# W products of both head parities in one burst, attention tiles in one PSUM ring, new ranks in the planner

## The chip, the cores and the metric

The kernel runs on one core of a Trainium2 chip. The metric is the device time of one execution in microseconds. Three runs of the kernel before took 285.99, 286.09 and 287.48 us; the median is 286.09 us.

## The reference, cut to what matters

There are 8 batches of 8 heads, 576 tokens and a head size of 64. In each head 32 "pack" queries first attend over the tokens, and the 576 token queries then attend over the 32 packed rows. Behind that stands an MLP with a gated activation:

```
p_packed = softmax(p @ k.T / 8) @ v              # 32 x 64 for each head
att      = softmax(q @ p_packed.T / 8) @ p_packed
x        = att, heads side by side               # 4608 x 512
h        = x @ w_in                              # 512 -> 2048
out      = (h * sigmoid(beta * h)) @ w_out       # 2048 -> 512
```

## The kernel before, in words

**Tiling.** Work goes batch by batch. The 8 heads are laid out as four columns c of two parities r: head 2c + r has partitions 64r to 64r + 63. The 576 tokens are split into 512 (main) and 64 (rest). The kernel never forms att: since p_packed is the value matrix of the second attention, att @ w_in equals the softmax weights times a small matrix W = p_packed @ w_in, which is 32 rows for each head, 256 rows by 2048 columns for a batch. So the MLP's first product has 256 rows to sum over instead of 512.

**Steps of one batch b**, with the names that the profile and the prediction use:

- k, q, v are loaded by SP (plan_loads) and cast to bf16 by POOL. `tr` transposes k and q on TensorE (tiles kT_ps, qT_ps), DVE copies them out (L279). `trr` and `rk`, `rq` do the same for the 64 rest tokens (remT_ps, L311, L313).
- `s1` and `s1r` are the scores of the pack queries (s1_ps, s1r_ps), `e1` their exp on ACT (L338, L357), `z1` the sums (z1_ps: a 128x64 tile of ones, once for each parity), `i1` the reciprocal on DVE (L390), `pun` the product with v (pp_ps), `pp` its scaling (L410).
- `s2` and `s2r` are the scores of the tokens against the packed rows, one tile for each parity (64x32 tiles of the array). `e2` is their exp (L450, L453), `z2` the sums (z2_ps), then ln and exp(-x) on ACT (L472, L474, L483) for the reciprocal, and `A2` the weights on DVE (L488).
- `w` is W: for each quarter n of the 2048 columns and each parity r, four matmuls of a 64x32 tile with 512 columns, one for each c, into one PSUM tile (w_ps). DVE multiplies it by beta into W_bf (`W`, L550, 0.68 us).
- `h` is W by A2 (two matmuls for each of 16 blocks ft, h_ps; `hr` for the rest tokens). ACT applies Silu (`g`, L578, L598).
- `o` is g by w_out in four tiles of 128 tokens, 16 matmuls each (o_ps), and a fifth for the rest tokens of two batches (g_rem). DVE copies each out (`take`, L636), and SP stores it.

In the profile all matmuls have line L164 and all transposes L169, the lines of two helpers; the tiles tell them apart. z1_ps and z2_ps are both shown as z_ps, s1_ps and s2_ps as s_ps.

**The order.** Every step is a Task with an engine, an assumed duration, what it depends on, and a rank. Planner.run plays the engines against assumed times, and emits on each free engine the ready task of lowest rank. The result is a fixed order for each engine. A task that opens a PSUM tile (`takes`) needs the oldest buffer of a ring to have been given back (`ends`). There are three rings: "h" with 2 buffers, "o" with 2 and "att" with 4. Before, h, hr, remT, s1r, z1 and pp share the ring "h", and all else of attention the ring "att". ACT has two table sets: exp (with ln) and silu. The rule for a switch is

```
if other and (mode == "silu" or not same) and not (mode == "exp" and soon):
```

where `other` are the tasks that could start now and need the other set, `same` those of the present set, and `soon` the exp tasks that come ready within 1.6 us. While the planner's clock is under 36 us (WARM_UNTIL), idle TensorE gets filler matmuls (warm_ps).

**Ranks before.** Attention of batch b has 100b + 5 to 100b + 12, h has 100b + 50, o has 100b + 260 and more. h(b) depends on the o tiles of batch b - 2, since g has two buffers.

Of the kernel before, what the change touches and what calls it, by code (L numbers as in the profile page):

```python
# [8 lines left out]
B, H, S, D = 8, 8, 576, 64  # L9
# [6 lines left out]
bf16 = mybir.dt.bfloat16  # L16
# [5 lines left out]
NC = 4  # L22
FT = DFF // 128
SM = 512
SR = 64
# [3 lines left out]
HOP_US = 0.2  # L29
LAND_US = 2.0  # L30
WARM_UNTIL = 36.0


class Task:

    __slots__ = ("engine", "us", "fn", "deps", "rank", "takes", "ends", "table", "end", "slot", "left", "ready", "users", "key")

    def __init__(self, engine, us, fn, deps, rank, takes, ends, table):  # L40
        self.engine, self.us, self.fn, self.deps, self.rank = engine, us, fn, deps, rank
        self.takes, self.ends, self.table = takes, ends, table
        self.end, self.slot, self.users, self.key = None, None, [], None
        self.left, self.ready = 0, 0.0


class Planner:
# [7 lines left out]

    def add(self, engine, us, fn, deps=(), rank=0, takes=None, ends=(), table=None):
        t = Task(engine, us, fn, [d for d in deps if d is not None], rank, takes, ends, table)
        self.tasks.append(t)
        return t

    def run(self):
# [9 lines left out]
        now, todo = 0.0, len(self.tasks)  # L71

        def room(t):
            if t.takes is None:
                return True
            n, opened = self.rings[t.takes]
            return len(opened) < n or (opened[-n][0] is not None and opened[-n][0] <= now + 1e-9)

        def start(t):
            nonlocal todo  # L80
            if t.takes is not None:
                t.slot = [None]
                self.rings[t.takes][1].append(t.slot)
            t.fn()
            t.end = now + t.us
            free[t.engine] = t.end
            for o in t.ends:
                o.slot[0] = t.end + HOP_US
            land = LAND_US if t.engine == "SP" else HOP_US
            for u in t.users:  # L90
                u.left -= 1
                u.ready = max(u.ready, t.end + (0.0 if u.engine == t.engine else land))
                if not u.left:
                    ready[u.engine].append(u)
            ready[t.engine].remove(t)
            todo -= 1

        while todo:
# [24 lines left out]
            if not moved:  # L123
                times = [x for x in free.values() if x > now + 1e-9]
                times += [t.ready for q in ready.values() for t in q if t.ready > now + 1e-9]
                times += [
                    o[-n][0] for n, o in self.rings.values() if len(o) >= n and o[-n][0] and o[-n][0] > now + 1e-9
                ]
                assert times, [(t.key, t.engine, room(t), t.ready - now) for q in ready.values() for t in q] + [[d.key for d in t.deps if d.end is None] for t in self.tasks if t.end is None and t.left][:9]
                now = min(times)  # L130


class Kernel:
# [128 lines left out]
    def plan_attention(self, b):  # L262
        nc = self.nc
        rank = 100 * b + 5
        st = self.t
# [18 lines left out]
        for x in "kq":  # L284
            old = [("s1", b - 1, i) for i in range(2)] if x == "k" else [("s2", b - 1, i) for i in range(3)]
            for i in range(2):
# [10 lines left out]
        def transpose_rest():  # L297
            st[b, "r", "ps"] = ps = self.ps_h.tile([128, 1024], bf16, tag="h", name="remT_ps")
            for xi, x in enumerate("kq"):
                for u in range(2):  # L300
                    self.tp(
                        ps[:, 256 * xi + 128 * u : 256 * xi + 128 * u + 128],
                        st[b, x][:, 2048 + 128 * u : 2048 + 128 * u + 128],
                        self.identr[:],
                    )

        def evacuate_rest(x):
# [11 lines left out]
            ("trr", b), "PE", 0.24, transpose_rest,  # L319
            [("cast", b, "k", 2), ("cast", b, "q", 2), ("s1r", b - 1), ("T", b, "q", 1)], rank + 1, takes="h",  # L320
        )
# [23 lines left out]
        def scores1_rest():  # L345
            st[b, "s1r"] = ps = self.bank("s1r_ps")
            for u in range(2):
# [6 lines left out]
        def exp1_rest():  # L354
# [4 lines left out]
        old = [("z1", b - 2), ("pun", b - 2)]  # L359
        s1r = self.task(("s1r", b), "PE", 0.12, scores1_rest, [("rk", b), ("pT",)] + old, rank + 2, takes="h")  # L360
        s1 = [
# [6 lines left out]
        e1 = [  # L368
            self.task(("e1", b, i), "ACT", 0.62, lambda i=i: exp1(i), [s1[i], s1r], rank + 2, ends=[s1[i]], table="exp")
            for i in range(2)  # L370
        ]
        e1.append(self.task(("e1r", b), "ACT", 0.56, exp1_rest, [s1r], rank + 2, ends=[s1r], table="exp"))
# [19 lines left out]
        def packed():  # L392
            st[b, "pun"] = ps = self.bank("pp_ps")
            v = st[b, "v"]
# [11 lines left out]
        def normalize1():  # L406
# [9 lines left out]

        z1 = self.task(("z1", b), "PE", 0.5, sums1, e1 + [("pp", b - 2)], rank + 3, takes="h")
        i1 = self.task(("i1", b), "DVE", 0.97, invert1, [z1], rank + 3, ends=[z1])
        old = [("s2", b - 2, i) for i in range(3)] + [("w", b - 2, n) for n in range(8)]
        pun = self.task(  # L420
            ("pun", b), "PE", 0.75, packed,
            e1 + [z1] + [("cast", b, "v", i) for i in range(3)] + old, rank + 4, takes="h",
        )
        self.task(("pp", b), "DVE", 0.6, normalize1, [i1, pun], rank + 4, ends=[pun])


        def scores2(i):
            st[b, "s2", i] = ps = self.att("s2_ps")
            for c in range(NC):
                self.mm(  # L430
                    ps[32 * c : 32 * c + 32, :],
                    st[b, "pp"][64 * i : 64 * i + 64, c, :],
                    st[b, "q", "T"][64 * i : 64 * i + 64, c, 0:SM],
                    pos=(64 * i, 32 * c),
                )

        def scores2_rest(r):
            st[b, "s2r", r] = ps = self.att("s2r_ps")
            for c in range(NC):
                self.mm(  # L440
                    ps[32 * c : 32 * c + 32, 0:SR],
                    st[b, "pp"][64 * r : 64 * r + 64, c, :],
                    st[b, "q", "T"][64 * r : 64 * r + 64, c, SM:S],
                    pos=(64 * r, 32 * c),
                )

# [48 lines left out]
        oldA = [("h", b - 2, ft) for ft in range(FT)] + [("hr", b - 2, 0), ("hr", b - 2, 1)]  # L495
        e2, s2r = [], []
        for i in range(2):
            s2 = self.task(("s2", b, i), "PE", 0.25, lambda i=i: scores2(i), [("pp", b), ("s2", b, i - 1)] + tq + oldE, rank + 5, takes="att")
            e2.append(
                self.task(  # L500
                    ("e2", b, i), "ACT", 0.62, lambda i=i: exp2(i), [s2] + e2[:1], rank + 5, ends=[s2], table="exp"
                )
            )
        for r in range(2):
            s2r.append(
                self.task(
                    ("s2", b, 2) if r else None, "PE", 0.1, lambda r=r: scores2_rest(r),
                    [("pp", b), ("rq", b), ("s2", b, 1)] + s2r + oldE, rank + 6, takes="att",
                )
            )  # L510
        e2r = [
            self.task(None, "ACT", 0.25, lambda r=r: exp2_rest(r), [s2r[r], e2[0]], rank + 6, ends=[s2r[r]], table="exp")
            for r in range(2)
# [19 lines left out]

        def fused_w(m):
            n, r = m // 2, m % 2
            st[b, "w", m] = ps = self.att("w_ps")
            for c in range(NC):
                self.mm(
                    ps[32 * c : 32 * c + 32, :],
                    st[b, "pp"][64 * r : 64 * r + 64, c, :],  # L540
                    self.w_in_bf[64 * r : 64 * r + 64, c, 512 * n : 512 * n + 512],
                    pos=(64 * r, 32 * c),
                )

# [8 lines left out]

        for m in range(8):
            w = self.task(
                ("w", b, m), "PE", 0.27, lambda m=m: fused_w(m),
                [("pp", b), ("w_in", m // 2), ("beta", m // 2), ("w", b, m - 1)] + oldA, rank + 7, takes="att",
            )
            self.task(("W", b, m), "DVE", 0.68, lambda m=m: scaled_w(m), [w, ("W", b, m - 1)], rank + 7, ends=[w])


    def plan_mlp(self, b):
        nc = self.nc
        st = self.t
        rank = 100 * b + 50

# [307 lines left out]
```

## Time and profile before

| | |
|---|---|
| median of three runs | 286.09 us |
| profiled execution | 285.96 us |
| its span, first to last instruction | 284.2 us |
| mean granted TensorE clock | 0.992 |
| TensorE (PE) busy | 269.2 us, 95% |
| ScalarE (ACT) busy | 151.5 us, 53% |
| VectorE (DVE) busy | 127.4 us, 45% |
| GpSimd (POOL) busy | 59.9 us, 21% |
| ACT table loads | 16 |

Times are microseconds unless marked ns. PE's busy time counts modelled ends, so what a matmul costs is read from the distance between starts. PEld is the weight load, which overlaps PE. In a row of groups stand: line, engine, operation, tile written and tiles read, shapes, count, then busy time and mean ns of one, and the idle time of the engine ahead of them with what ended most of it. In a timeline row stand: start, length, engine, line, operation, tiles, shapes, count, and in brackets a wait ahead of it.

### The profile page before, as it was taken

How to read it: one execution, taken by the hardware profiler on the slowest of the kernel's cores; microseconds unless marked ns; L12 is line 12 of the kernel's file. 1: busy time of each engine (PE TensorE's matmuls, PEld its weight loads, DVE VectorE, ACT ScalarE, POOL GpSimd, SP SyncE). 2: the span in 40 equal slices, each digit the busy share in tenths (PEclk: the TensorE clock that was granted, in tenths of full speed). 3: DMA queues.
4: the chain of work that ended last, by engine and by line, in shares of the span. 5: the costliest groups of instructions: out<-in, count | busy, mean ns of one | idle time of the engine just before them, and what ended most of it. 6: DMA issues, size and time to landing. Idle time of an engine off the chain costs nothing.

```text
span 284.2 us, 5670 instructions
## 1 busy us (share of the span) xinstructions
PE 269.2 (95%) x2382; PEld 138.8 (49%) x2382; DVE 127.4 (45%) x232; ACT 151.5 (53%) x280; POOL 59.9 (21%) x58
## 2 busy tenths in 40 slices
PE   7957999999999999999999999999999999989993
PEld 6954555345553446444553446434563445524441
DVE  6636536893156504581146502492055802381110
ACT  1637476626638465636627467355646366387500
POOL 4117560143081006300170005400063000000000
PEclk9999799999999999999999999999999999999999
DMA  6999999989939701991149510791021011100022
GB/s 217 303 350 367 299 327 379 319 238 317 290 112 294 214 37 40 256 311 44 39 145 325 178 40 37 228 334 52 0 76 70 9 35 38 75 37 2 10 101 74
DMA packets 47737, 47.02 MB, mean 165 GB/s; under 512 B 14289, under 2 KB 38881, under 8 KB 47713
## 3 DMA queue, kind: packets, MB, share of 16 engines
q1 hardware_dynamic: 47712, 46.68, 54.2%
q8 instruction: 18, 0.29, 0.5%
q14 instruction: 7, 0.05, 0.1%
HBM read 37.23 MB, written 9.44 MB: 164 GB/s over the span
## 4 chain that ended last, share of the span: by engine, by line
PE 76%; DMA 13%; DVE 5%; SPq 3%; POOL 1%; issue 1%; POOLq 0%; DVEq 0%
PE o_ps L164 42%; PE h_ps L164 17%; PE w_ps L164 5%; DMA w_out<-in_moe_w_out_dram 4%; DMA q<-in_q_dram 4%; DMA w_in<-in_moe_w_in_dram 3%; PE hr_ps L164 2%; DMA k<-in_k_dram 2%; PE z_ps L164 2%; PE s_ps L164 2%; PE qT_ps L169 2%; PE kT_ps L169 2%; DVE o_sb L636 2%; SPq L219 2%; DVE A2T L488 1%; PE pp_ps L164 1%
## 5 line engine op out<-in xcount | busy, mean ns | idle before, releaser
L164 PE MATMUL o_ps<-w_out_bf,g_main 128*128 128x512 bf16 x512 | 131.9, 380 | 0.7 <-DVE o_sb L636 0.3
L578 ACT ACTIVATE g_main<-h_ps 128x512 bf16<-128x512 f32 x128 | 71.2, 595 | 59.4 <-PE h_ps L164 59.1
L164 PEld LDWEIGHTS <-g_main 128*128 128x128 bf16 x512 | 45.2, 98 | 52.1 <-issue 9.0
L164 PE MATMUL h_ps<-A2T,W_bf 128*128 128x512 bf16 x256 | 69.1, 382 | 0.4 <-ACT g_main L578 0.4
L636 DVE COPY o_sb<-o_ps 128x512 f32<-128x512 f32 x36 | 24.5, 688 | 95.5 <-PE o_ps L164 95.5
L550 DVE TENSOR_TENSOR W_bf<-w_ps,beta_bc 128x512 bf16<-128x512 f32 x64 | 40.6, 684 | 19.6 <-PE w_ps L164 19.6
L164 PEld LDWEIGHTS <-W_bf 128*128 128x128 bf16 x512 | 32.2, 98 | 30.2 <-issue 5.4
L239 POOL CAST k_bf<-k 128x2048 bf16<-128x2048 f32 x7 | 13.3, 1893 | 119.7 <-PE remT_ps L169 105.4
L450 ACT ACTIVATE E2T<-s_ps 128x512 bf16<-128x512 f32 x16 | 8.7, 595 | 35.9 <-PE s2r_ps L164 29.2
L164 PE MATMUL w_ps<-w_in_bf,pp 64*32 64x512 bf16 x256 | 21.5, 393 | 3.1 <-POOL w_in_bf L786 1.6
L179 ACT ACT_TABLE_LOAD x16 | 20.5, 1283 | 1.0 <-PEq L858 0.7
L164 PEld LDWEIGHTS <-pp 64*32 64x32 bf16 x384 | 6.9, 89 | 27.5 <-issue 23.1
L164 PE MATMUL warm_ps<-identr 128*128 128x128 bf16 x165 | 15.0, 244 | 1.9 <-DVE bones L681 1.9
L239 POOL CAST v_bf<-v 128x2048 bf16<-128x2048 f32 x7 | 13.3, 1893 | 15.1 <-issue 8.4
L164 PE MATMUL o_ps<-w_out_bf,g_rem 128*128 128x512 bf16 x64 | 16.1, 380 | 0.0
L279 DVE COPY kT<-kT_ps 128x1024 bf16<-128x1024 bf16 x15 | 9.8, 685 | 11.5 <-PE kT_ps L169 11.5
L488 DVE TENSOR_TENSOR A2T<-E2T,rz 128x512 bf16<-128x512 bf16 (+1 forms) x24 | 14.7, 648 | 0.2 <-ACT rz L483 0.2
L164 PEld LDWEIGHTS <-identr 128*128 128x128 bf16 x165 | 12.2, 111 | 4.9 <-DVE bones L681 1.9
L239 POOL CAST q_bf<-q 128x2048 bf16<-128x2048 f32 x7 | 13.3, 1893 | 2.8 <-DMA q<-in_q_dram 2.8
L483 ACT ACTIVATE rz<-rz 128x512 f32<-128x512 f32 (+1 forms) x24 | 12.6, 523 | 0.8
L598 ACT ACTIVATE g_rem<-hr_ps 128x512 bf16<-128x512 f32 x16 | 8.9, 595 | 4.8 <-PE hr_ps L164 4.8
L169 PEld LDWEIGHTS <-k_bf 128*128 128x128 bf16 x144 | 9.4, 98 | 3.9 <-issue 0.3
(67 smaller groups left out, 205.1 us busy)
## 6 DMA issues: line engine op xcount, KB each, us to landing
out_dram<-o_sb SPq DMA_DIRECT2D x32, 256.0 KB, 2.4
k<-in_k_dram SPq DMA_DIRECT2D x7, 1024.0 KB, 6.7
q<-in_q_dram SPq DMA_DIRECT2D x7, 1024.0 KB, 8.4
v<-in_v_dram SPq DMA_DIRECT2D x7, 1024.0 KB, 7.8
w_in<-in_moe_w_in_dram SPq DMA_DIRECT2D x4, 1024.0 KB, 9.9
w_out<-in_moe_w_out_dram SPq DMA_DIRECT2D x4, 1024.0 KB, 8.3
k<-in_k_dram SPq DMA_DIRECT2D x2, 512.0 KB, 5.5
k<-in_k_dram SPq DMA_DIRECT2D x16, 64.0 KB, 6.3
```

Source lines behind the costliest of these rows:

```text
L164: return self.nc.tensor.matmul(out, lhsT, rhs, start=start, stop=stop, tile_position=pos, skip_group_check=True)
L169: return self.nc.tensor.matmul(out, in_, ident, is_transpose=True, skip_group_check=True)
L179: self.nc.scalar.preload_act_table_set(SETS[mode])
L239: self.copy[engine](o[:, 0:2048].rearrange("p (t h d) -> p h t d", t=4, h=8)[:, h], t[:, 0:2048].rearrange("p (h t d) -> p h t d", h=8, t= ...
L279: self.copy[engine](st[b, x, "T"][:, 2 * i : 2 * i + 2, 0:SM], st[b, x, "ps", i][:].rearrange("p (c n) -> p c n", c=2),)
L450: nc.scalar.activation(st[b, "E2"][:, i, 0:SM], st[b, "s2", i][:], AF.Exp, scale=SCALE)
L483: nc.scalar.activation(rz, rz, AF.Exp, scale=-1.0)
L488: nc.vector.tensor_tensor(part(st[b, "A2"], i), part(st[b, "E2"], i), part(st[b, "rz2"], i), ALU.mult)
L550: nc.vector.tensor_tensor(st[b, "W"][:, r, cols], st[b, "w", m][:], self.beta_bc[:, cols], ALU.mult)
L578: nc.scalar.activation(st[b, "g"][:, ft, :], st[b, "h", ft][:], AF.Silu)
L598: nc.scalar.activation(st[b // 2, "gr"][:, 8 * half : 8 * half + 8, o : o + 64], st[b, "hr", half][:].rearrange("p (f n) -> p f n", f=8), ...
L636: nc.vector.tensor_copy(o[:], st[b, "o", t][:])
```

## The change

- `w` becomes one task for each quarter n (WN = 1), which takes two buffers of the ring (`count=2`) and issues eight matmuls, parities alternating inside each c. Each of the two buffers is given back by its own evacuation `W`.
- `s2` becomes one task for both parities with two buffers, and `s2r` likewise, also with the parities alternating.
- The ten matmuls of `z1` alternate between the parities, where all five of one came before all five of the other.
- The tiles of `trr`, `s1r`, `z1` and `pun` move from the ring "h" to the ring "att", which keeps four buffers. Only h and hr (and two small tiles at the start) are left in "h".
- `e1` of batch b waits for the first `e2` of batch b - 1, from batch 2 on.
- Attention's ranks go from 100b + 5 to 100b - 30, those of h from 100b + 50 to 100b - 300. s2r has rank + 5 instead of + 6.

The planner's ring test looks at `count` buffers, and a task can end one buffer of several. The diff, cut to its core:

```diff
 def room(t):
-    return len(opened) < n or (opened[-n][0] is not None and opened[-n][0] <= now + 1e-9)
+    for i in range(len(opened) - n, len(opened) - n + t.count):
+        if i >= 0 and (opened[i][0] is None or opened[i][0] > now + 1e-9):
+            return False
+    return True
...
 def plan_attention(self, b):
-    rank = 100 * b + 5
+    rank = 100 * b - 30
...
-    st[b, "r", "ps"] = ps = self.ps_h.tile([128, 1024], bf16, tag="h", name="remT_ps")
+    st[b, "r", "ps"] = ps = self.att("remT_ps", bf16)
...
-    st[b, "s1r"] = ps = self.bank("s1r_ps")
+    st[b, "s1r"] = ps = self.att("s1r_ps")
...
-    self.task(("e1", b, i), "ACT", 0.62, lambda i=i: exp1(i), [s1[i], s1r], rank + 2, ends=[s1[i]], table="exp")
+    self.task(("e1", b, i), "ACT", 0.62, lambda i=i: exp1(i), [s1[i], s1r, ("e2", b - 1, 0) if b > 1 else None], rank + 2, ends=[s1[i]], table="exp")
...
 def sums1():
-    st[b, "z1"] = ps = self.bank("z1_ps")
-    for r in range(2):
-        for t in range(5):
+    st[b, "z1"] = ps = self.att("z1_ps")
+    for t in range(5):
+        for r in range(2):
...
-    st[b, "pun"] = ps = self.bank("pp_ps")
+    st[b, "pun"] = ps = self.att("pp_ps")
...
-def fused_w(m):
-    n, r = m // 2, m % 2
-    st[b, "w", m] = ps = self.att("w_ps")
+def fused_w(n):
+    for r in range(2):
+        st[b, "w", 2 * n + r] = self.att("w_ps")
     for c in range(NC):
-        self.mm(ps[32 * c : 32 * c + 32, :], ...
+        for r in range(2):
+            self.mm(st[b, "w", 2 * n + r][32 * c : 32 * c + 32, :], ...
...
-for m in range(8):
+for n in range(0, 4, WN):
     w = self.task(
-        ("w", b, m), "PE", 0.27, lambda m=m: fused_w(m),
-        [("pp", b), ("w_in", m // 2), ("beta", m // 2), ("w", b, m - 1)] + oldA, rank + 7, takes="att",
-    )
-    self.task(("W", b, m), "DVE", 0.68, lambda m=m: scaled_w(m), [w, ("W", b, m - 1)], rank + 7, ends=[w])
+        ("w", b, n), "PE", 0.15 + 0.25 * WN, lambda n=n: [fused_w(n + i) for i in range(WN)],
+        [("pp", b), ("w", b, n - WN)] + [(x, n + i) for x in ("w_in", "beta") for i in range(WN)] + oldA,
+        rank + 7, takes="att", count=2 * WN,
+    )
+    for i in range(2 * WN):
+        m = 2 * n + i
+        self.task(("W", b, m), "DVE", 0.68, lambda m=m: scaled_w(m), [w, ("W", b, m - 1)], rank + 7, ends=[(w, i)])
...
 def plan_mlp(self, b):
-    rank = 100 * b + 50
+    rank = 100 * b - 300
```

More of the change, by code (lines that the diff above doesn't have):

```diff
@@ L31, with __init__ @@
 WARM_UNTIL = 36.0
+WN = 1
 class Task:
-    __slots__ = ("engine", "us", "fn", "deps", "rank", "takes", "ends", "table", "end", "slot", "left", "ready", "users", "key")
-    def __init__(self, engine, us, fn, deps, rank, takes, ends, table):
+    __slots__ = ("engine", "us", "fn", "deps", "rank", "takes", "count", "ends", "table", "end", "slot", "left", "ready", "users", "key")
+    def __init__(self, engine, us, fn, deps, rank, takes, count, ends, table):
         self.engine, self.us, self.fn, self.deps, self.rank = engine, us, fn, deps, rank
-        self.takes, self.ends, self.table = takes, ends, table
+        self.takes, self.count, self.table = takes, count, table
+        self.ends = [e if isinstance(e, tuple) else (e, 0) for e in ends]
         self.end, self.slot, self.users, self.key = None, None, [], None
@@ L54, in __init__, with add @@
         self.switch, self.filler = switch, filler
-    def add(self, engine, us, fn, deps=(), rank=0, takes=None, ends=(), table=None):
-        t = Task(engine, us, fn, [d for d in deps if d is not None], rank, takes, ends, table)
+    def add(self, engine, us, fn, deps=(), rank=0, takes=None, count=1, ends=(), table=None):
+        t = Task(engine, us, fn, [d for d in deps if d is not None], rank, takes, count, ends, table)
         self.tasks.append(t)
@@ L81, in start @@
             if t.takes is not None:
-                t.slot = [None]
-                self.rings[t.takes][1].append(t.slot)
+                t.slot = [[None] for _ in range(t.count)]
+                self.rings[t.takes][1].extend(t.slot)
             t.fn()
@@ L86, in start @@
             free[t.engine] = t.end
-            for o in t.ends:
-                o.slot[0] = t.end + HOP_US
+            for o, i in t.ends:
+                o.slot[i][0] = t.end + HOP_US
             land = LAND_US if t.engine == "SP" else HOP_US
@@ L284, in plan_attention @@
         for x in "kq":
-            old = [("s1", b - 1, i) for i in range(2)] if x == "k" else [("s2", b - 1, i) for i in range(3)]
+            old = [("s1", b - 1, i) for i in range(2)] if x == "k" else [("s2", b - 1, i) for i in range(2)]
             for i in range(2):
@@ L319, in plan_attention @@
             ("trr", b), "PE", 0.24, transpose_rest,
-            [("cast", b, "k", 2), ("cast", b, "q", 2), ("s1r", b - 1), ("T", b, "q", 1)], rank + 1, takes="h",
+            [("cast", b, "k", 2), ("cast", b, "q", 2), ("s1r", b - 1), ("T", b, "q", 1)], rank + 1, takes="att",
         )
@@ L359, in plan_attention @@
         old = [("z1", b - 2), ("pun", b - 2)]
-        s1r = self.task(("s1r", b), "PE", 0.12, scores1_rest, [("rk", b), ("pT",)] + old, rank + 2, takes="h")
+        s1r = self.task(("s1r", b), "PE", 0.12, scores1_rest, [("rk", b), ("pT",)] + old, rank + 2, takes="att")
         s1 = [
@@ L495, in plan_attention @@
         oldA = [("h", b - 2, ft) for ft in range(FT)] + [("hr", b - 2, 0), ("hr", b - 2, 1)]
[L496 to L510, printed above, removed]
+        s2 = self.task(
+            ("s2", b, 0), "PE", 0.3, lambda: scores2("s2", 0, SM), [("pp", b)] + tq + oldE, rank + 5, takes="att", count=2
+        )
+        e2 = [
+            self.task(("e2", b, i), "ACT", 0.62, lambda i=i: exp2(i), [s2], rank + 5, ends=[(s2, i)], table="exp")
+            for i in range(2)
+        ]
+        s2r = self.task(
+            ("s2", b, 1), "PE", 0.14, lambda: scores2("s2r", SM, S),
+            [("pp", b), ("rq", b), s2] + oldE, rank + 5, takes="att", count=2,
+        )
         e2r = [
-            self.task(None, "ACT", 0.25, lambda r=r: exp2_rest(r), [s2r[r], e2[0]], rank + 6, ends=[s2r[r]], table="exp")
+            self.task(None, "ACT", 0.25, lambda r=r: exp2_rest(r), [s2r, e2[0]], rank + 6, ends=[(s2r, r)], table="exp")
             for r in range(2)
```

49 lines of the change are left out of this document (20 added, 29 removed).

## The prediction

> **What bounds the kernel now.** I read the page first, for the span and the busy shares.
>
> ```profile
> span 284.2 us, 5670 instructions
> ## 1 busy us (share of the span) xinstructions
> PE 269.2 (95%) x2382; PEld 138.8 (49%) x2382; DVE 127.4 (45%) x232; ACT 151.5 (53%) x280; POOL 59.9 (21%) x58
> ```
>
> The profiled execution took 285.96 us, 1.76 us more than its span and 0.13 us less than the median of 286.09 us; the sum below is made against 285.96. TensorE is the candidate, but its busy share is modelled, so the next view is the table of windows, one window per batch in the middle of the run (columns: window, its length, then busy time and count of PE, PEld, DVE, ACT, POOL; granted clock; DMA share; GB/s).
>
> ```profile
> 60.00:93.00 33.00, 33.00 (x298) 16.24 (x299) 16.86 (x30) 19.18 (x36) 10.31 (x10) 1.00 0.89 252
> ...
> 191.00:224.00 33.00, 32.87 (x280) 15.80 (x279) 13.85 (x26) 17.94 (x35) 6.66 (x6) 1.00 0.15 50
> ```
>
> PE has no gap in these windows and its clock is full (1.00), while ACT works 18 to 19 of 33 us and DVE 14 to 17. So over the middle of the run the time is what the PE instructions cost, one behind the other, and a microsecond taken out of PE comes off the end, provided PE still finds work. What each of them costs is read from the starts in the PE timeline (start, length, instruction, count), not from the lengths.
>
> ```profile
> 151.84 0.40 PE L164 MATMUL w_ps<-w_in_bf,pp 64*32 64x512 bf16 x4
> 152.17 1.04 PE L164 MATMUL o_ps<-w_out_bf,g_main 128*128 128x512 bf16 x4
> 153.14 0.40 PE L164 MATMUL w_ps<-w_in_bf,pp 64*32 64x512 bf16 x4
> 153.47 1.04 PE L164 MATMUL o_ps<-w_out_bf,g_main 128*128 128x512 bf16 x4
> 154.44 0.41 PE L164 MATMUL w_ps<-w_in_bf,pp 64*32 64x512 bf16 x8
> 154.78 1.04 PE L164 MATMUL o_ps<-w_out_bf,g_main 128*128 128x512 bf16 x4
> 155.75 0.40 PE L164 MATMUL w_ps<-w_in_bf,pp 64*32 64x512 bf16 x4
> ...
> 160.44 1.03 PE L164 MATMUL o_ps<-w_out_bf,g_rem 128*128 128x512 bf16 x4
> 161.30 1.03 PE L164 MATMUL h_ps<-A2T,W_bf 128*128 128x512 bf16 x4
> ```
>
> Four full-array matmuls that are left alone take 161.30 - 160.44 = 0.86 us, so one pass of 512 columns is 0.216 us. The four W products of one head parity (64x32 tiles side by side) hold PE for 152.17 - 151.84 = 0.33 us, a pass and 0.11 us more, and the four o matmuls ahead of the next burst take 153.14 - 152.17 = 0.97, another 0.11 us over 0.86. A burst of one parity thus costs 0.44 us for 0.216 us of streaming; the rest is paid at its two edges. The burst of eight at 154.44 happens to hold both parities, and takes 0.34 us (to 154.78) with the same edge of 0.11 after it (155.75 - 154.78 = 0.97): 0.45 us for twice the work. That is the saving the change can have.
>
> **The W bursts.** I counted the bursts in the PE timeline from the first W product of batch 1 to the last of batch 6; these are the two ends of the list.
>
> ```profile
> 54.13 0.40 PE L164 MATMUL w_ps<-w_in_bf,pp 64*32 64x512 bf16 x4
> ...
> 223.51 0.40 PE L164 MATMUL w_ps<-w_in_bf,pp 64*32 64x512 bf16 x4
> ```
>
> There are 41: 35 of four, 5 of eight and one of twelve. Their cost is 35 x 0.44 = 15.40, 5 x 0.45 = 2.25, and 0.45 + 0.216 = 0.67 for the twelve: 18.3 us. After the change each batch has four bursts of eight: 24 x 0.45 = 10.8. Gain 7.5 us, all on the path as PE has no gap there. If the planner places two pairs back to back when the ring is empty, two edges (0.22 us) go per such place: at one a batch another 1.3 us, the low end. What is new is that parities alternate inside the burst, which no row shows. If each pair of row halves ran one after the other, a burst would take a pass more: 24 x 0.216 = 5.2 us back; below nothing it can't go, since a burst of eight already runs in one pass. I take 0.45, since the nearest row (154.44) has all eight tiles at work at once.
>
> Batch 7 is apart, because PE has little o work left to put between its bursts:
>
> ```profile
> 249.71 0.45 PE L164 MATMUL w_ps<-w_in_bf,pp 64*32 64x512 bf16 x8
> 250.91 0.50 PE L164 MATMUL w_ps<-w_in_bf,pp 64*32 64x512 bf16 x8 [0.75 <-ACT rz L472]
> 251.74 0.87 PE L164 MATMUL w_ps<-w_in_bf,pp 64*32 64x512 bf16 x8 [0.33 <-ACT rz L474]
> 252.55 1.08 PE L164 MATMUL h_ps<-A2T,W_bf 128*128 128x512 bf16 x4
> 253.62 0.40 PE L164 MATMUL w_ps<-w_in_bf,pp 64*32 64x512 bf16 x4
> 254.22 0.40 PE L164 MATMUL w_ps<-w_in_bf,pp 64*32 64x512 bf16 x4 [0.20 <-DVE W_bf L550]
> 254.55 1.04 PE L164 MATMUL h_ps<-A2T,W_bf 128*128 128x512 bf16 x4
> ```
>
> From 249.71 to 254.55 are 4.84 us, of which 0.86 is the four h matmuls; 3.98 us go to W products and to waits (0.75 + 0.33 + 0.20 = 1.28) for the ring. Afterwards attention of batch 7 no longer waits for the h ring, so it falls into the time of silu(6), where o work covers it: 4 x 0.45 = 1.8, a gain of 2.2 us (from 0.9 with the waits left to 2.2). Batch 0 gains nothing: its W products wait for w_in.
>
> **z1 and s2.** These are the rows of one batch.
>
> ```profile
> 178.70 0.55 PE L164 MATMUL z_ps<-E1T,ones 128*64 128x128 bf16 x10
> 179.18 0.76 PE L164 MATMUL pp_ps<-E1T,v_bf 128*128 128x64 bf16 x20
> ...
> 181.60 0.41 PE L164 MATMUL s_ps<-qT,pp 64*32 64x512 bf16 x8
> 181.82 0.21 PE L164 MATMUL s2r_ps<-qT,pp 64*32 64x64 bf16 x8
> 181.97 1.04 PE L164 MATMUL o_ps<-w_out_bf,g_main 128*128 128x512 bf16 x4
> ```
>
> The ten z1 matmuls take 0.48 us. Ten passes of 128 columns in a row would be 10 x 0.054 + 0.11 = 0.65, five pairs 5 x 0.054 + 0.11 = 0.38: the two halves overlap already, so the new order can bring 0.10 a batch at most and lose 0.17 if it breaks the overlap; I take half the gain, 0.4 us in eight batches (from -1.4 to 0.8). The eight s2 products run already in one pass (181.82 - 181.60 = 0.22), with s2r right behind: nothing to gain, and 0.22 us a batch to lose (two more edges, 1.5 us in seven) if s2r must wait for its two buffers and o work comes between. I take nothing, because z1 and pun give their buffers back before s2 can start.
>
> **The ring, the ranks and the tables.** remT, s1r, z1 and pp move from the two h buffers to the ring of four, and h gets the lowest rank numbers. No instruction is added, and W needs two free buffers at once, which DVE empties one after the other. The costs are in waits. Behind a waiting W burst on PE stand h, o and attention of the next batch; behind W's evacuation on DVE stand i1, pp, A2 and the o copies. I cost them at nothing because the o matmuls of a batch (64 x 0.216 = 13.8 us) are ready by then; their price without that cover is a rival below. ACT gets nothing from shared tables that would show:
>
> ```profile
> L578 ACT ACTIVATE g_main<-h_ps 128x512 bf16<-128x512 f32 x128 | 71.2, 595 | 59.4 <-PE h_ps L164 59.1
> L179 ACT ACT_TABLE_LOAD   x16 | 20.5, 1283 | 1.0 <-PEq L858 0.7
> ```
>
> There are 16 loads, the first and two a batch less one at the end. An exp stretch and a silu stretch per batch stay, so 16 is about the least afterwards too; and ACT sits 59.1 us waiting for h from PE. The Trainium skill ("ScalarE: Activation LUTs", What ACT_TABLE_LOAD costs) puts a switch at about 2.66 us with a drain; the rows here have 1.283 us, and by the page's price the sum stays as it is, for no load goes. What does move is the gap inside one exp stretch:
>
> ```profile
> 182.05 1.08 ACT L450 ACTIVATE E2T<-s_ps 128x512 bf16<-128x512 f32 x2 [5.10 <-PE s2r_ps L164]
> ...
> 186.19 1.28 ACT L179 ACT_TABLE_LOAD   x1
> ```
>
> ACT waited 5.10 us there between the first and the second softmax of the same batch. With e1 of the next batch behind e2 this gap falls away, which shortens ACT's chain, not PE's work. Of the queues that work is moved past, SP's loads and POOL's casts come due some us earlier; POOL waits 105.4 us for transposes ahead of k casts, so the data is there long before:
>
> ```profile
> L239 POOL CAST k_bf<-k 128x2048 bf16<-128x2048 f32 x7 | 13.3, 1893 | 119.7 <-PE remT_ps L169 105.4
> ```
>
> The first 44 us are set by loads, which stay: the first o matmuls wait for this cast and its DMA.
>
> ```profile
> 43.57 1.68 DVE L796 TENSOR_SCALAR w_out_bf<-w_out,rbeta 128x512 bf16<-128x512 f32 x4 [3.07 <-DMA w_out<-in_moe_w_out_dram]
> ```
>
> Attention of batch 1 may slip into PE's free time before that (a gain of about 1 us), or its table switch may hold up the last silus of batch 0 (two loads of 1.283, a loss of up to 2.6 us); I take nothing.
>
> **The sum.** 7.5 + 2.2 + 0.4 = 10.1 us; 285.96 - 10.1 = 275.9, and 276.0 against the median.
>
> **The rivals.** First, *evacuation takes over*:
>
> ```profile
> L550 DVE TENSOR_TENSOR W_bf<-w_ps,beta_bc 128x512 bf16<-128x512 f32 x64 | 40.6, 684 | 19.6 <-PE w_ps L164 19.6
> ```
>
> DVE needs 2 x 0.684 = 1.37 us per pair, and the ring now also carries four more tiles a batch. Where PE waits in each of batches 1 to 6 as it does in batch 7 (1.28 us), 7.7 us come back: 283.7. Against it: DVE is under half busy and the middle windows have no PE gap even with single bursts. The Trainium skill ("TensorEngine Tiling (Array Packing)", PSUM Bottleneck) says that packing speeds the array and not the emptying of PSUM, which can then become the bound; this case's trace shows it only in batch 7. A part of these waits, 2 to 5 us, gives 278 to 281. Second, *the alternating parities serialise*: 276.0 + 5.2 = 281.2. Against it speaks the row at 154.44.
>
> Third, slower: *the table ping-pong*. The rule in Planner.run leaves silu mode as soon as any exp task can start. With s1r, z1 and pp out of the h ring, e1 or s2 of the next batch can come ready in the middle of silu(b); ACT then loads exp, does its 4.1 us (182.05 to 186.19), and loads silu. If e1 and e2 come at different times, that is two loads (2.57 us) more per batch, and h stands still meanwhile. PE feels it only when the o work runs out. It decides from 10.1 / 7 = 1.44 us uncovered per batch; with all of 2.57 uncovered in seven batches, 18 us come back: 294. For it: the old order kept the two stretches apart by the h ring, and the new one has only e1's wait on e2. Against it: ACT has 59.1 us of slack, and a stop of 6.7 us is under the 13.8 us of o work. Fourth, *nothing moves*, because ACT's chain of switches and waits sets the period once PE is lighter: about 285.9.
>
> **How the numbers follow.** The forecast (274.5 to 277.5) has 0.46. Below it 0.14: pairs back to back at two places a batch (2.6) and an early batch 1 (1.0) reach 272.4. A part of the waits, or s2r apart, 0.18; serialised 0.03; evacuation in full 0.05; nothing moves 0.02; slower by ping-pong 0.12. The range 272.4 to 283.8 leaves out the last two and little besides. Half a per cent, 1.4 us, is about what a measurement can tell here. Faster takes all the cases that end below 284.7, 0.86; same 0.02; slower 0.12.
>
> **What would show it.** Right: W products of batches 1 to 6 in bursts of eight, 0.34 us from start to next start; no PE gap in windows of about 31.5 us a batch; 16 to about 20 table loads; z1 at 0.38 to 0.48. Wrong: PE waits on W_bf or on s and z tiles' readers in the chain of waits (evacuation), bursts of 0.55 (serialised), 28 or more table loads with PE waits on g_main (ping-pong), or a last h batch that starts no sooner.

## The result, and the profile after

The changed kernel takes 276.62 us (median of four, 275.46 to 278.71), beside 286.39 us for the kernel before in the same session: a ratio of 0.966 (95% interval 0.959 to 0.973). Forecast were 276.0 us and a range of 272.4 to 283.8. The total was right. The experiments show that the reason given for it was only half of the mechanism.

The profiled execution took 278.71 us, the slowest of the four, so it shows 7.25 us less than the profile of before and not the 9.8 us between the medians. First come the page's head and two windows from the middle (window, its length, busy time and count of PE, PEld, DVE, ACT, POOL; granted clock; DMA share; GB/s):

```profile
span 276.8 us, 5707 instructions
PE 260.0 (94%) x2394; PEld 138.7 (50%) x2394; DVE 131.8 (48%) x232; ACT 173.0 (62%) x296; POOL 60.6 (22%) x58
...
60.00:93.00 33.00, 33.00 (x332) 17.23 (x331) 21.58 (x37) 25.91 (x43) 14.21 (x12) 1.00 1.00 271
...
191.00:224.00 33.00, 33.00 (x286) 15.53 (x270) 16.36 (x29) 23.07 (x43) 1.00 (x2) 1.00 0.11 41
```

PE is as full as before, at full clock in these windows, but ACT now works 23 to 26 of 33 us where it worked 18 to 19. Now z1 and two W bursts in the timeline of PE (start, length, instruction, count):

```profile
125.33 0.47 PE L167 MATMUL z_ps<-E1T,ones 128*64 128x128 bf16 x10
125.74 0.76 PE L167 MATMUL pp_ps<-E1T,v_bf 128*128 128x64 bf16 x20
...
132.57 0.41 PE L167 MATMUL w_ps<-w_in_bf,pp 64*32 64x512 bf16 x8
132.91 1.90 PE L167 MATMUL o_ps<-w_out_bf,g_main 128*128 128x512 bf16 x8
134.74 0.41 PE L167 MATMUL w_ps<-w_in_bf,pp 64*32 64x512 bf16 x8
135.08 1.25 PE L167 MATMUL o_ps<-w_out_bf,g_main 128*128 128x512 bf16 x5
```

A pair takes 132.91 - 132.57 = 0.34 us and the edge behind it 134.74 - 132.91 - 8 x 0.216 = 0.10: 0.44 us, as forecast. Batches 1 to 6 hold 24 such bursts and no other. z1 takes 0.41 us where it took 0.48.

What was not forecast is on ACT. Groups (busy us, mean ns, then idle us before them and what ended most of it), and a stretch of ACT's timeline:

```profile
L182 ACT ACT_TABLE_LOAD x32 | 41.1, 1283 | 1.3 <-PEq L853 0.7
L573 ACT ACTIVATE g_main<-h_ps 128x512 bf16<-128x512 f32 x128 | 71.2, 595 | 46.5 <-PE h_ps L167 46.0
```

```profile
120.98 0.60 ACT L573 ACTIVATE g_main<-h_ps 128x512 bf16<-128x512 f32 x1 [0.43 <-PE h_ps L167]
121.59 1.28 ACT L182 ACT_TABLE_LOAD   x1
122.89 0.55 ACT L360 ACTIVATE E1T<-s1r_ps 64x128 bf16<-64x128 f32 x2
123.47 1.08 ACT L341 ACTIVATE E1T<-s_ps 128x512 bf16<-128x512 f32 x2
124.57 1.28 ACT L182 ACT_TABLE_LOAD   x1
125.86 1.09 ACT L573 ACTIVATE g_main<-h_ps 128x512 bf16<-128x512 f32 x2
127.39 1.08 ACT L573 ACTIVATE g_main<-h_ps 128x512 bf16<-128x512 f32 x2 [0.45 <-PE h_ps L167]
128.50 1.28 ACT L182 ACT_TABLE_LOAD   x1
129.79 1.09 ACT L445 ACTIVATE E2T<-s_ps 128x512 bf16<-128x512 f32 x2
```

The table loads doubled, from 16 to 32. The first softmax of the next batch breaks into the silus of this one, then the second does, each with a load on both sides. This is the ping-pong that the prediction described, and it costs the path nothing visible: PE waits for no g_main after 50 us (its one named wait from there on is 1.7 us for an o copy), and ACT's waiting for h falls from 59.1 to 46.0 us. In return attention runs ahead. The end of the run:

```profile
221.55 0.41 PE L167 MATMUL w_ps<-w_in_bf,pp 64*32 64x512 bf16 x8
221.89 1.90 PE L167 MATMUL o_ps<-w_out_bf,g_main 128*128 128x512 bf16 x8
223.72 0.41 PE L167 MATMUL w_ps<-w_in_bf,pp 64*32 64x512 bf16 x8
...
227.23 0.63 PE L167 MATMUL w_ps<-w_in_bf,pp 64*32 64x512 bf16 x16
...
243.37 1.10 PE L167 MATMUL hr_ps<-A2T,W_bf 128*128 128x64 bf16 x32
```

Batch 7 has its W at 221.55 (249.71 before), inside the silus of batch 6 and without a wait, and its last h products at 243.37 (266.2 before). Behind them 128 o matmuls run to the end in one row.

**An account of PE's time.** From the first o matmul to the last, I priced every instruction by its start-to-start time (0.216 us for a pass of 512 columns and so on), each W pass at 0.216 and each change of the tile shape at 0.11. Matmuls whose record is missing from a trace (25 of the 512 o products of g_main in `pairs_only`) are counted in. The rest is what is left over; I read it as waiting and lowered clock.

| kernel | first to last o | full-array and score work | W passes | changes of shape | rest |
|---|---|---|---|---|---|
| before | 235.2 | 206.7 | 46: 9.9 | 114: 12.5 | 6.1 |
| after | 226.6 | 207.2 | 28: 6.0 | 84: 9.2 | 4.1 |
| pairs_only | 239.8 | 207.6 | 28: 6.0 | 72: 7.9 | 18.2 |
| ring_only | 230.2 | 207.5 | 38: 8.2 | 92: 10.1 | 4.5 |
| ring_old | 236.0 | 207.1 | 28: 6.0 | 68: 7.5 | 15.3 |
| one_stretch | 229.1 | 207.1 | 28: 6.0 | 78: 8.6 | 7.4 |
| ranks_old | 224.5 | 207.2 | 28: 6.0 | 78: 8.6 | 2.7 |

From before to after, passes bring 3.9 us, edges (the changes of shape) 3.3, and the rest 2.0. The first o matmul came 1.2 us later in this execution (45.3 against 44.1), which takes part of it back.

### The profile page after: what moved, and what is told of

Read it like the earlier page. It is cut to its first block, busy times and chain, and to the rows that moved or that the text cites. A ratio compares the mean times of both kernels' runs of the same rounds, so it can differ in the third digit from the quotient of the medians.

```text
span 276.8 us, 5707 instructions
## 1 busy us (share of the span) xinstructions
PE 260.0 (94%) x2394; PEld 138.7 (50%) x2394; DVE 131.8 (48%) x232; ACT 173.0 (62%) x296; POOL 60.6 (22%) x58
## 4 chain that ended last, share of the span: by engine, by line
PE 86%; DVE 5%; DMA 3%; ACT 2%; SPq 1%; issue 0%; POOL 0%; POOLq 0%; DVEq 0%
PE o_ps L167 45%; PE h_ps L167 18%; PE w_ps L167 3%; DMA w_out<-in_moe_w_out_dram 3%; PE hr_ps L167 3%; PE kT_ps L172 2%; PE qT_ps L172 2%; PE z_ps L167 2%; PE warm_ps L167 2%; PE s_ps L167 2%; DVE A2T L483 2%; PE pp_ps L167 2%; PE brow_ps L167 2%; SPq L222 1%; DVE W_bf L542 1%; DVE identr L672 1%
## 5 line engine op out<-in xcount | busy, mean ns | idle before, releaser
L167 PE MATMUL o_ps<-w_out_bf,g_main 128*128 128x512 bf16 x512 | 125.6, 381 | 3.8 <-DVE w_out_bf L791 2.0
L167 PEld LDWEIGHTS <-g_main 128*128 128x128 bf16 x512 | 46.9, 98 | 57.2 <-issue 8.5
L167 PE MATMUL h_ps<-A2T,W_bf 128*128 128x512 bf16 x256 | 69.9, 381 | 1.2 <-DVE W_bf L542 1.1
L483 DVE TENSOR_TENSOR A2T<-E2T,rz 128x512 bf16<-128x512 bf16 (+1 forms) x24 | 17.4, 753 | 6.1 <-ACT rz L478 6.0
L167 PE MATMUL w_ps<-w_in_bf,pp 64*32 64x512 bf16 x256 | 13.0, 386 | 0.5 <-POOL w_in_bf L781 0.5
L393 DVE RECIPROCAL rz<-z_ps 128x128 f32<-128x128 f32 x8 | 7.6, 955 | 10.5 <-PE z_ps L167 10.5
L167 PEld LDWEIGHTS <-pp 64*32 64x32 bf16 x384 | 4.9, 88 | 15.4 <-issue 11.0
```

What stands on the lines that cost most here:

```text
L167: return self.nc.tensor.matmul(out, lhsT, rhs, start=start, stop=stop, tile_position=pos, skip_group_check=True)
L393: nc.vector.reciprocal(rz[:], st[b, "z1"][:, 0:128])
L483: nc.vector.tensor_tensor(part(st[b, "A2"], i), part(st[b, "E2"], i), part(st[b, "rz2"], i), ALU.mult)
```

## The experiments

Ratios are to the kernel before, run on the same chip in the same session, with 95% intervals. Diffs are shortened. Times of a chain run from one named start to the next in PE's timeline.

### The pairs without the new ring

`pairs_alone` puts the ranks, the h ring's four tiles, e1 and z1 back. It keeps the change's paired tasks for s2 and s2r (issued one parity behind the other, as before); the expectation, which says that s2 is as before, overlooked that, so `pairs_only` below repeats it without them.

```diff
-    rank = 100 * b - 30
+    rank = 100 * b + 5
-    rank = 100 * b - 300
+    rank = 100 * b + 50
-    ps = self.att("remT_ps", bf16)        # and s1r, z1, pp: takes="att"
+    ps = self.ps_h.tile(..., tag="h")     # takes="h"
-    e1: [s1[i], s1r, ("e2", b - 1, 0)]
+    e1: [s1[i], s1r]
```

> The kernel before, with the W products alone fused to pairs (two buffers, one burst of eight); rings, ranks, e1's dependence, s2, z1 as before. Bursts theory (the gain is the edges of the W bursts on a full PE): 41 bursts in batches 1 to 6 become 24, 18.3 - 10.8 = 7.5 us less, about 278.5 us against 286, with 16 table loads. Order theory (the gain is what the new ring and ranks bring, attention running ahead into silu): 284 to 286 us.

Measured: 290.49 us, ratio 1.012 (1.008 to 1.016), 16 loads. That is above what either theory expected. The pairs alone bring nothing and cost a little.

### The new ring and order without the pairs

`no_pairs` keeps all of the change but the W pairs: `for m in range(8)`, one parity and one buffer for each task, as before.

> The changed kernel with the W products back in eight tasks of one parity each; rings, ranks, e1's dependence, s2 and z1 as changed. Bursts theory: about 7 us given back, 283 to 285 us, though the planner issues 30 table loads. Order theory: 276 to 278 us, as the changed kernel.

Measured: 285.34 us, ratio 0.992 (0.989 to 0.995), 30 loads, just above what the bursts theory expected (283 to 285). With the new ring in place the pairs are thus worth what was forecast for them: from 0.992 to 0.966 are 7.4 of 286.4 us. Neither half brings what both bring together, so the gain is no sum of parts.

### How the pair is issued

`parity_outer` issues the four tiles of one parity ahead of the other's (`for r` outside `for c`); `wn2` sets `WN = 2`, so that a W task takes all four buffers and issues 16 matmuls.

> The changed kernel, but within a W burst all four columns of parity 0 come before those of parity 1, the order that the burst of eight in the kernel before had. Bursts theory: a burst keeps 0.34 us and the time stays within 0.5% of the changed kernel (275.3 to 278). Rival (alternating is what makes the two halves of the array run together): 0.2 us more a burst, 6 us in all, 282 us.

> The changed kernel with WN = 2: two bursts of sixteen a batch, each taking all four buffers. Bursts theory: two pairs of edges fewer a batch, 2 x 0.22 x 7 = 3.1 us less, 273.5 us. Rival (evacuation bounds the ring): all four buffers must be empty at once and DVE needs 4 x 0.68 = 2.7 us to empty them, so PE waits or attention is pushed late: 277 to 282 us.

Measured: `parity_outer` 277.14 us, 0.964 (0.959 to 0.968), with bursts of eight in 0.34 us as well, so the alternation is worth nothing here. `wn2` 277.85 us, 0.967 (0.961 to 0.972), in the range of its rival. Its bursts of 16 take 0.56 us, and 26 fewer changes of shape than in the changed kernel should save 2.9 us. Most of that is lost in one place of its trace: the burst at 83.90 us holds PE until 86.73, since two of its tiles come free late (waits of 0.32 and 0.23 us) and PE then waits 1.00 us for DVE to empty the ring; from 87.0 to 90.4 us the granted clock is 0.50. Here too edges saved are not time saved.

### The new order with the old ring

`ring_old` puts only the four tiles back into the h ring (the ring lines of the diff above). Pairs, ranks, e1's wait and z1 stay.

> The changed kernel with remT, s1r, z1 and pp back in the h ring of two; pairs, ranks and e1's dependence as changed. The planner then keeps both softmaxes of a batch in one exp stretch (16 table loads, as before). Bursts theory (the saved edges come off whatever the order): 276 to 278 us. Order theory (new, after the pairs alone brought nothing: with one exp stretch a batch, its chain from e1 to A2 sets the period once PE is lighter, and the saved time becomes waits on PE): 285 to 291 us.

Measured: 289.07 us, 1.006 (1.003 to 1.009), 16 loads. It has the fewest changes of shape of the table (68) and a rest of 15.3 us. Of the 3.2 us by which its profiled execution is longer than that of before, 2.5 are a later first o matmul (46.6 us against 44.1), but the 8.9 us of passes and edges that it saves are gone. So the ring is what the pairs need.

### The ranks, and e1's wait

`ranks_old` puts both rank lines back and nothing else; `no_dep` takes e1's wait on `("e2", b - 1, 0)` out of the changed kernel.

> The changed kernel with the ranks of before (attention 100b + 5, h 100b + 50); pairs, ring and e1's dependence as changed. The planner issues 32 table loads, as in the changed kernel. Order theory: the ranks are not what matters, 276 to 278.5 us. Rival (the ranks free PE): 282 us and more.

> The changed kernel without e1's wait on e2 of the batch before, which was to bring both softmaxes under one table load. Theory 1 (the wait brings nothing: with the four tiles out of the h ring the exp stretches break into silu with or without it, about 31 loads either way, and o work covers them): ratio 0.960 to 0.973, the changed kernel's 0.966 within it. Theory 2 (the wait saves ACT time that counts): ratio over 0.976.

Measured: `ranks_old` 276.01 us, 0.961 (0.957 to 0.966), 32 loads; `no_dep` 277.40 us, 0.970 (0.964 to 0.975), 32 loads. Neither matters. The part of the change that was to bring two softmaxes under one load brings no load less, since the exp tasks break into silu either way.

### Attention kept out of silu

`one_stretch` is the changed kernel with remT waiting for the last h of the batch before, which restores one exp stretch a batch.

```diff
-    [..., ("s1r", b - 1), ("T", b, "q", 1)], rank + 1, takes="att"
+    [..., ("s1r", b - 1), ("T", b, "q", 1), ("hr", b - 1, 1)], rank + 1, takes="att"
```

> The changed kernel, with trr made to wait for the second hr of the batch before. Ring, ranks and pairs stay as changed, but attention can no longer enter silu, so ACT has both softmaxes of a batch in one exp stretch and 16 table loads. Order theory: about as the ring put back, 285 to 291 us, with half of the table loads. Rival (the room in the h ring is what matters, not the order on ACT): 276 to 279 us. Tables theory (fewer loads are worth 16 x 1.28 us of ACT): under 276 us.

Measured: 281.04 us, 0.981 (0.976 to 0.985), 16 loads. It lies between the ranges of the order theory and of its rival, and half the loads make it no faster, so the tables theory falls. This splits the gain. With the pairs and the new ring, but without running ahead, 1.9% is won. Letting attention into silu, at twice the loads, wins the other 1.5%.

### What table loads cost

`loads_twice` puts a load of a third set ahead of each load (and tells the planner 2.6 us for a switch, so its order changes too).

```diff
+    self.nc.scalar.preload_act_table_set("sqrt_and_others")
     self.nc.scalar.preload_act_table_set(SETS[mode])
```

> The changed kernel with every table switch made of two loads (a third set in between), the planner told 2.6 us a switch; 76 loads against 32, 44 x 1.28 = 56 us more work on ACT, whose waits for h were 46 us. PE-bound theory: most of it goes into ACT's waits, 277 to 282 us. Rival (ACT's loads already lie on the path, as in the ping-pong rival of the prediction): 295 us and more.

Measured: 323.96 us, 1.126 (1.118 to 1.134). Groups and windows:

```profile
L182 ACT ACT_TABLE_LOAD x38 | 48.8, 1283 | 1.3 <-PEq L854 0.7
L183 ACT ACT_TABLE_LOAD x38 | 48.8, 1283 | 0.2
```

```profile
60.00:92.00 32.00, 26.22 (x256) 14.37 (x255) 16.95 (x29) 28.14 (x40) 10.02 (x10) 0.82 0.97 269
92.00:124.00 32.00, 24.08 (x237) 13.30 (x237) 11.86 (x23) 29.08 (x40) 13.31 (x12) 0.71 0.58 166
```

The PE-bound theory (277 to 282 us) fails here. 76 loads, 44 more than in the changed kernel, are 44 x 1.283 = 56.5 us of ACT, and about 46 us came through (1.126 against 0.966). ACT is the fullest engine in these windows (28 to 29 of 32 us), and PE has gaps. So the changed kernel's 32 loads are covered, but its cover, 23 to 26 us of ACT in 33, does not hold 44 more; where it ends was not measured. PE's granted clock falls as well (0.82 and 0.71); more on that below.

### Pairs and ring, each alone from the kernel before

`pairs_only` is the kernel before with the W pairs and nothing else, `ring_only` the kernel before with the four tiles moved to the ring "att" and nothing else.

> The kernel before with the W products in pairs and nothing else: s2 and s2r are single tasks as before, and so are the h ring's four tiles, the ranks, z1 and e1. Theory 1 (with remT, s1r, z1 and pp in the two h buffers, one batch's chain through ACT and PE is as long as the batch's PE work, so PE time that is saved becomes waiting): ratio 0.995 to 1.015, 16 table loads, PE waits of 10 us or more in all between 60 and 220 us. Theory 2 (the prediction's: 0.22 us saved per burst come straight off, 7.5 us in all): ratio 0.970 to 0.978.

> The kernel before with remT, s1r, z1 and pp in the ring of four instead of the h ring, and nothing else: single W products, the old s2 tasks, ranks, z1 order, and e1 without its wait on e2. Theory 1 (the ring lets attention run ahead, but the PE time is still that of single W bursts, so PE is full and little is won): ratio 0.985 to 1.000, over 28 table loads, PE full in the middle windows. Theory 2 (the ring's run-ahead is the gain by itself, the pairs bring little): ratio under 0.975. Theory 3 (over 30 loads cost what they last, 1.28 us each on the path): ratio over 1.03.

Measured: `pairs_only` 289.57 us, 1.012 (1.008 to 1.016), 16 loads; `ring_only` 282.13 us, 0.986 (0.981 to 0.991), 40 loads. The ring alone is 1.4% faster, the pairs alone 1.2% slower, and both in the changed kernel 3.4% faster. The other theories fall. The waits of 10 us or more that were expected between 60 and 220 us are put too high: those that the trace names come to 8.7 us from 60 to 260. By the account 4.1 of the 5.0 us that `ring_only` saves are passes (1.7) and edges (2.4), so most of its gain is the forecast's own mechanism, W bursts that grow longer.

PE's waits in `pairs_only` from 60 to 260 us (total, times, longest), then PE's timeline in batch 3 and two rows of DVE's:

```profile
PE h_ps L167 <- ACT g_main L585: 4.3, 6, 0.9
PE w_ps L167 <- DVE W_bf L554: 3.3, 7, 1.7
```

```profile
126.39 0.63 PE L167 MATMUL w_ps<-w_in_bf,pp 64*32 64x512 bf16 x16
...
128.14 0.66 PE L167 MATMUL w_ps<-w_in_bf,pp 64*32 64x512 bf16 x8
128.73 0.61 PE L167 MATMUL h_ps<-A2T,W_bf 128*128 128x512 bf16 x2
129.59 0.39 PE L167 MATMUL w_ps<-w_in_bf,pp 64*32 64x512 bf16 x1 [0.25 <-DVE W_bf L554]
130.19 0.41 PE L167 MATMUL w_ps<-w_in_bf,pp 64*32 64x512 bf16 x7 [0.21 <-DVE W_bf L554]
130.53 0.60 PE L167 MATMUL h_ps<-A2T,W_bf 128*128 128x512 bf16 x2
131.82 0.38 PE L167 MATMUL h_ps<-A2T,W_bf 128*128 128x512 bf16 x1 [0.69 <-ACT g_main L585]
133.09 1.01 PE L167 MATMUL h_ps<-A2T,W_bf 128*128 128x512 bf16 x2 [0.90 <-ACT g_main L585]
133.90 1.06 PE L167 MATMUL o_ps<-w_out_bf,g_main 128*128 128x512 bf16 x2
134.75 1.06 PE L167 MATMUL h_ps<-A2T,W_bf 128*128 128x512 bf16 x2
135.61 0.79 PE L167 MATMUL o_ps<-w_out_bf,g_main 128*128 128x512 bf16 x2
136.23 0.59 PE L167 MATMUL h_ps<-A2T,W_bf 128*128 128x512 bf16 x2
136.66 0.59 PE L167 MATMUL o_ps<-w_out_bf,g_main 128*128 128x512 bf16 x2
```

```profile
128.26 0.68 DVE L643 COPY o_sb<-o_ps 128x512 f32<-128x512 f32 x1
128.86 3.67 DVE L554 TENSOR_TENSOR W_bf<-w_ps,beta_bc 128x512 bf16<-128x512 f32 x6
```

From 128.14 to 133.90 us PE puts no o matmuls between. It waits for DVE, which empties six W tiles in a row without a gap (3.67 us), then for ACT, which has to give back the h buffers. Before, the first W burst came 1.0 us after the first z2 (149.97 to 150.98); here, with two buffers to be had at once, it comes 3.6 us after (122.8 to 126.4), and o work filled the time in between. W then is bound by its evacuation, with nothing left to cover it. I read the serial chain of a batch (last h, remT, s1, e1, z1, pp, s2, e2, z2, W, first h) as what sets the period: from hr to hr, batches 3 to 6 take 32.2 to 32.4 us where they took 32.0 to 33.2 before. That keeps 1.8 us of the PE time saved in these four batches. Batch 2 loses 5.4 (36.3 against 30.9): there W meets a DVE that is full for 8 us (the third busy time in these windows), and silu waits 4.2 and 4.6 us for h. The profiled execution is 4.3 us longer than that of before, so this one batch decides its total. That the chain sets the period is not shown, and one number speaks against it: batch 2 of the kernel before, with the same ring, takes 30.9 us.

```profile
92.00:96.00 4.00, 3.23 (x22) 1.28 (x20) 4.00 (x6) 0.21 (x1) 1.90 (x1) 1.00 1.11 275
96.00:100.00 4.00, 3.84 (x25) 1.66 (x25) 3.99 (x9) 0.60 (x1) 2.59 (x3) 1.00 0.83 233
```

Why the ring would lift this, which is argued and not shown: with remT, s1r, z1 and pp out of the two h buffers, they no longer wait for silu to give these back. Attention of the next batch starts in the middle of silu, so its serial steps lie beside h and o work. The stretch from hr to z2 is shorter already in `one_stretch`, which starts attention right behind the last h: 9.4 us (109.2 to 118.6), where before has 11.2 (138.8 to 150.0) and `ring_old` 11.4 (142.6 to 154.0). But `pairs_only`, with the old ring, has 9.2 (145.7 to 155.0) and is slow all the same, so this stretch does not tell the two rings apart. What does is the rest in the account: 15.3 and 18.2 us for the pairs with the old ring, 2.7 to 7.4 in the four kernels of the table with the new one. `ring_only` also shows the planner making long bursts by itself, since W finds an empty ring:

```profile
157.47 0.40 PE L167 MATMUL w_ps<-w_in_bf,pp 64*32 64x512 bf16 x4
...
160.55 0.61 PE L167 MATMUL w_ps<-w_in_bf,pp 64*32 64x512 bf16 x12
...
162.92 0.62 PE L167 MATMUL w_ps<-w_in_bf,pp 64*32 64x512 bf16 x16
```

It has 22 bursts in batches 1 to 6, where the kernel before has 41.

### A version that could beat both

`outer_ranks` joins the two small gains, the old ranks and the parities one behind the other.

> A version that may beat the changed kernel: the changed kernel with the old rank numbers (which gave 0.961) and with all four column tiles of one parity ahead of those of the other in a W burst (which gave 0.964). Theory 1 (both are the same to PE, and what is left is startup and the mode edges): ratio 0.958 to 0.968, no better than either. Theory 2 (both small gains are real and add up): ratio under 0.958.

Measured: 276.66 us, 0.966 (0.963 to 0.969). It does not beat the changed kernel, and `ranks_old` (0.961, 0.957 to 0.966) can't be told from it either: its interval overlaps with that of the change.

## Why the prediction was right, and where it was not

- **W bursts, -7.5 us.** The size is right: 24 bursts at 0.44 to 0.45 us, and with the new ring the pairs are worth 7.4 us (`no_pairs`). That it comes off the end because PE has no gap was argued from a necessary condition only. By the account `pairs_only` saves more of it than the change does (3.9 us of passes and 4.6 of edges, against 3.9 and 3.3), and it is 1.2% slower, because the rest grows by 12.1 us. The same reasoning gave 278.5 us for `pairs_alone`, which took 290.49. So part of the hit is luck: the sum holds because the change brought the ring along, and the forecast had not asked whether the pairs need it.
- **Batch 7, -2.2 us.** Right. Its bursts cost 0.45 + 0.45 + 0.67 = 1.6 us against 3.98, and the waits of 1.28 us are gone, for the reason given.
- **z1, -0.4 us.** Right: 0.07 us in each of batches 2 to 7, 0.4 us, most of the 0.10 that was possible. In batch 1 of this execution it took 0.68 us; the granted clock is 0.59 from 46 to 50 us. s2 and s2r split in only one batch.
- **The ring at nothing outside batch 7.** This is the step that failed. The ring is the condition for all the rest: without it the change is 0.6% slower than the kernel before (`ring_old`), and alone it brings 1.4%. The ranks and e1's wait at nothing were right.
- **"16 is about the least afterwards too".** That was wrong: 32. The text also held the right mechanism, the ping-pong, but as a mishap. It is the price of running ahead, and running ahead is worth 1.5% (`one_stretch`). Of the sign named for it, 28 or more loads with PE waits on g_main, only the first half came: the o work covered the stops, as the prediction judged.
- **"Nothing moves", chance 0.02.** For the change it did not come. For the pairs with the old ring it did, in three kernels (1.006 to 1.012), but that ACT's chain is the reason is not shown: in `pairs_only` the named waits are 4.3 us for ACT and 3.6 for DVE. The forecast did not name that rival's condition, which is the ring that remT, s1r, z1 and pp share with h.
- **Evacuation.** The Trainium skill ("TensorEngine Tiling (Array Packing)", PSUM Bottleneck) warned that the emptying of PSUM can become the bound. The rows of `pairs_only` agree (3.67 us of DVE without a gap, PE waiting); in the changed kernel, where o work lies between the bursts, it does not decide.
- **The price of a switch.** The Trainium skill ("ScalarE: Activation LUTs", What ACT_TABLE_LOAD costs) puts a switch at about 2.66 us. The rows have 1.283 us with 0.02 us on either side (121.59 to 122.89), and 16 more loads raised ACT's busy time by 173.0 - 151.5 = 21.5 us, 1.34 each. The measurement decides.
- **"31.5 us a batch"** has no row to answer to it: first h to first h is 28.0 us on average in batches 1 to 7 (61.9 to 229.6), because the o work is put off to the end. `one_stretch`, which does not run ahead, has the forecast's period (94.1 to 125.6 to 157.1, 31.5 us each).

What stays open: the share of the 1.2 us of later start that is chance, whether `ranks_old` is truly faster by the 0.2% of its median, and how the ring lets the saved PE time through. Pairs and ring were not run together without the ranks, e1's wait, z1 and the paired s2; the ranks and e1's wait were taken back one at a time, z1's order and the paired s2 never alone.

## What to carry to other kernels

A full engine does not prove that work taken out of it comes off the end: 8.5 and 8.9 us of passes and edges saved on PE came back in the rest in `pairs_only` and `ring_old`. Before such a saving is forecast, ask which waits stand right behind it, and look for the buffers that tie the next round's start to this round's end; moving a few small tiles out of a shared ring made a saving count that was worth nothing without it. More table loads can be the cheaper order, as long as the engine that they stop has slack and the engine behind it has other work.

## What the runs showed of the hardware that was not expected

- **TensorE's clock fell behind gaps of under 1 us, though not each time.** In `pairs_only`, after waits of 0.25, 0.21, 0.69 and 0.90 us within 4 us, two matmuls take 0.81 to 0.86 us (133.09 to 135.61) where two take 0.43 from 136.23 on. The granted clock of 132 to 136 us is 0.57:

```profile
128.00:132.00 4.00, 2.85 (x22) 0.82 (x22) 4.00 (x8) 1.19 (x2) 3.79 (x4) 1.00 0.41 134
132.00:136.00 4.00, 3.10 (x8) 1.11 (x8) 0.92 (x3) 1.34 (x3) 0.00 (x0) 0.57 0.83 259
136.00:140.00 4.00, 4.00 (x20) 1.86 (x19) 0.00 (x0) 2.78 (x5) 0.00 (x0) 1.00 1.11 312
```

  The eight matmuls from 133.09 to 136.23 take 3.14 us where eight take 4 x 0.43 = 1.72 behind them: 1.4 us more, behind 2.05 us of gaps. The Trainium skill ("TensorE: Matmul & The Clock Gate", Why this matters for your kernels) advises against idle gaps over about 3 us; here the clock fell behind gaps of under 1 us, close together, and the measurement decides. The same repeats at 196 to 200 us (0.68), and `loads_twice` has 0.82 and 0.71 over 32 us each (0.91 to 0.93 as the mean of each of its four executions). But such gaps alone do not decide it: in the kernel before PE is as empty from 250 to 254 us (2.84 of 4 us, waits of 0.75, 0.33 and 0.20), and in `pairs_only` emptier from 253 to 257 (2.59 of 4), and the clock stays at 1.00 there and in the 4 us behind. What makes the difference is not shown.
- **Order inside a packed burst.** Four 64x32 tiles of one parity ahead of the other four, or alternating, take the same 0.34 us for eight (in `parity_outer` 22 of the 24 bursts of batches 1 to 6, the other two 0.57; `no_dep`, which alternates, has two such as well). For the 128x64 tiles of z1 the order did matter: 0.48 us one half behind the other, 0.41 alternating.
